# Two layers of attention, mixer and MLP on one core: layer 1 split into a shorter last pair of chunks, value products on four column tiles, late outputs repacked by TensorE

## The chip, the cores and the metric

The kernel runs on one core of a Trainium2 chip. The metric is device time of one execution in microseconds (us); the kernel before takes 1644.31 us (median of 3 runs, 1643.47 to 1644.97). A change of less than 2% counts as "the same". The core's granted TensorE clock was 0.994 to 1.0 of full speed in each profile that the text compares.

## The reference, cut to what matters

```python
def reference(A_x, A_wq, A_wk, A_wv, A_wo, B_x, B_w1, B_w2, B_w3, B_w4):
    # S = 2048 tokens, D = 512, H = 32 query heads of 16, ONE key and value head
    # A: softmax(q k / 4) v, then wo        B: a token-shifting mixer (w1, gelu, shift, w2)
    #                                          and an MLP (w3, gelu, w4) of width 1792
    x = A_x
    x = x + _A_ref(_layernorm(x), A_wq, A_wk, A_wv, A_wo)      # layer 1, attention
    x = x + _B_ref(_layernorm(x), B_w1, B_w2, B_w3, B_w4)      # layer 1, mixer and MLP
    x = x + _A_ref(_layernorm(x), A_wq, A_wk, A_wv, A_wo)      # layer 2, same weights
    x = x + _B_ref(_layernorm(x), B_w1, B_w2, B_w3, B_w4)
    return x
```

Each layer needs 32 x 2048 x 2048 exponentials, which is 1024 units of 128 x 1024, 2048 for both layers. All of layer 1's tokens have to be finished before the last keys of layer 2 exist.

## The kernel before

The program is written by a scheduler that runs when the kernel is built. Operations are declared with what they read and write, an assumed duration and a priority; the scheduler fixes the order in which each engine executes them. The order is then frozen: nothing is decided on the chip. So most of the class constants below are not sizes of the computation but settings of that scheduler.

Queries go in *chunks* of up to four tiles of 128. While the attention of one chunk runs, the *side work* of the chunk before it (output projection, mixer, MLP, keys and queries for layer 2) runs between the attention products. An attention unit has a score product on TensorE (PE), an exponential of 128 x 1024 on ScalarE (ACT, written to `EA`), and a value product on PE. To relieve ACT some units are done by VectorE (DVE) instead. Such a *pair* costs two conversions from PSUM (where TensorE's products land) into the integer tile `J`, two shifted copies `JK`, and three value products:

```python
    # declare_pair (cut)
            o = op("DVE", lambda e, i=i, L=L: e.tensor_scalar(
                out=J[:, i * 512:(i + 1) * 512], in0=self.PB[:, L.bank, :],
                scalar1=128 * LOG2E * 0.25, scalar2=float(127 * 128), op0=ALU.mult, op1=ALU.add), ...)
        for k in (1, 2):
            eng = "POOL" if len(self.adds) < self.ADDS else "DVE"        # ADDS = 0: always DVE
            x = op(eng, lambda e, k=k, r=r: e.tensor_scalar(
                out=self.JK[:, r, :], in0=J, scalar1=float(self.STEPS[k]), scalar2=1.0, ...), ...)
```

A pair is granted while the order is made, when a score product is placed, if enough of the three shared PSUM banks are free and DVE is not behind:

```python
    def attach(self, q):
        if sum(1 for t, b in self.pl.pool if t + 0.06 <= self.pl.now) >= self.FREE:     # FREE = 2
            self.assign(self.pl.now, 1 - q.pe[3][0] // 2)
    # assign (cut): no grant if DVE is too far behind
        if self.pl.backlog() > self.BACKLOG or ...                                      # BACKLOG = 6
```

Value products and most side products use PE in the same tiling (one `pe_kind`), score products in another. While PE is in the first, a side product of that kind gets the priority `STICK` (-1: ahead of everything, unless a due score product would become late), although value products have priority 2 and side products mostly 10:

```python
            if stick and o.prio > 2 and o.pe[0] == self.pe_kind and not any(... > x for x in due):
                key = (self.STICK, o.seq)
```

The value product of a unit, in the kernel before: two heads, each on its own column tile of 32, 512 columns each. `CHUNKS` gives each chunk as (first tile, tiles); `URGE` gives the priority of each chunk's side work, `PACE` spreads that work over time:

```python
    CHUNKS = (((0, 4), (4, 4), (8, 4), (12, 4)),              # layer 1
              ((0, 4), (4, 4), (8, 4), (12, 2), (14, 2)))     # layer 2
    # declare_pv (cut)
                for i in range(2):
                    h = 2 * p + i
                    ins = e.matmul(self.PB[32 * h:32 * h + 32, self.ACC, 0:w], lhsT=v[:, la, kb + j, :],
                                   rhs=ap[:, i, j * w:(j + 1) * w], ..., tile_position=(0, 32 * h))
```

The softmax here doesn't subtract the row's maximum and nothing guards it: scores larger than these inputs give would overflow.

## Time and profile before

| | before | read from |
|---|---|---|
| median time | 1644.3 us | runs |
| exponentials on ACT, and pairs on DVE | 1545 and 503 | groups of instructions (1006 conversions J, two a pair) |
| ACT, DVE, POOL, PE busy | 94%, 86%, 6%, 99% | page, first part |
| start of the first exponential | 19.6 us | trace |
| lost between exponentials | 47.2 us | worked out, see below |
| end of the last exponential to the end (the tail) | 59.0 us | trace |

The lines of these views stand in the prediction. "Lost" is worked out from the trace for each two exponentials that follow one another on ACT: the time from start to start, less 0.917 us (the pitch of an undisturbed row of them), less the GELUs and table loads that lie between (before a GELU, and again before the next exponential, ACT loads a table, 1.28 us each). Added up by stretch it shows where ACT had nothing to do. Because the order is frozen, the number of exponentials can be counted without running anything; how much is lost can't.

The same view by stretch for all engines will be used again. Its columns are the stretch, its length, and for PE, PE's weight loads, DVE, ACT and POOL the busy time (and instructions), then the granted clock, the DMA share and GB/s. Before, in the quiet stretch where only attention runs, and in the one that holds most of the border:

```profile
41.00:205.00 164.00, 163.22 (x1732) 46.41 (x1728) 150.71 (x308) 164.00 (x181) 0.00 (x0) 1.00 0.04 8
...
780.00:960.00 180.00, 175.99 (x2343) 62.17 (x2341) 146.80 (x325) 151.02 (x156) 16.53 (x25) 1.00 0.01 2
```

In the first ACT is never idle. In the second, at the border of the layers, it is idle for 29 us of 180. The longest, on PE and then on ACT:

```profile
789.70 6.43 PE L607 MATMUL PB<-W,G 128*32 128x512 bf16 x116
```
```profile
796.38 30.38 ACT L997 ACTIVATE EA<-PB 128x1024 bf16<-128x1024 f32 x33 [9.64 <-PE PB L1075]
```

PE did MLP products in a row (from 787.31; the first fence shows the part in the view from 790 us), the value products that free EA came after them, and then 33 exponentials ran without a wait. So here ACT did not lack keys or queries: its buffers were full, because side products went ahead of value products. The second longest wait, 7.6 us up to 865.74, has 144 products of the MLP's first layer on PE in the same way.

### The profile page before, as it was taken

To read this page: it belongs to the slowest core of one execution; us is meant where nothing else is said; L and a number is where in the kernel's file an instruction comes from. 1 tells how busy PE (TensorE), PEld (TensorE's weight loads), DVE (VectorE), ACT (ScalarE), POOL (GpSimd) and SP (SyncE) were. 2 spreads that over 40 slices of the span, in tenths; PEclk is the share of its full clock that TensorE was granted. 3 is DMA by queue.
4 is the path that set the end of the run, shared out by engine and by line. 5 is a ranking of instruction groups with operands and counts; after the bars stand their busy time and mean duration, and the time that the engine had idled before them with its cause. 6 is when DMAs were issued, how large, how long until landed. Compare 5 with 4: busy or idle time off the path is not lost.

```text
span 1641.6 us, 47631 instructions
## 1 busy us (share of the span) xinstructions
PE 1617.8 (99%) x21141; PEld 545.5 (33%) x21141; DVE 1414.8 (86%) x2978; ACT 1535.7 (94%) x1623; POOL 105.6 (6%) x162
## 2 busy tenths in 40 slices
PE   8999999999999999999999999999999999999999
PEld 3222223322332223233333332333223223444454
DVE  8999999889999789898986798998899987899853
ACT  4999999999999999999797999999999999999952
POOL 3000000000010001100120000010000000010001
PEclk9999999999999999999999999999999999999999
DMA  6000000000100000100000000000000000000000
GB/s 204 17 4 4 5 18 5 5 3 5 18 5 3 5 3 5 18 5 5 2 2 2 2 8 8 5 18 4 14 11 4 4 5 11 19 5 5 6 17 18
DMA packets 24398, 20.79 MB, mean 13 GB/s; under 512 B 7168, under 2 KB 23680, under 8 KB 24192
## 3 DMA queue, kind: packets, MB, share of 16 engines
q1 hardware_dynamic: 24192, 17.75, 4.1%
q8 instruction: 165, 2.70, 0.7%
q14 instruction: 41, 0.34, 0.1%
HBM read 7.90 MB, written 2.10 MB: 6 GB/s over the span
## 4 chain that ended last, share of the span: by engine, by line
ACT 75%; PE 22%; DVE 2%; DMA 0%; POOL 0%; issue 0%; SPq 0%; POOLq 0%
ACT EA L997 70%; PE PB L607 10%; PE PB L953 6%; PE PB L1075 5%; ACT G L1364 2%; ACT L997 1%; ACT GP L1288 1%; ACT L1288 1%; PE PB L773 1%; ACT L1364 0%; DVE ST L713 0%; DVE G L1357 0%; DVE ZR L756 0%; DMA X<-in_A_x_dram 0%; POOL X L1371 0%; DVE J L1018 0%
## 5 line engine op out<-in xcount | busy, mean ns | idle before, releaser
L997 ACT ACTIVATE EA<-PB 128x1024 bf16<-128x1024 f32 x1545 | 1423.2, 1084 | 58.4 <-PE PB L1075 34.1
L1018 DVE TENSOR_SCALAR J<-PB 128x512 uint16<-128x512 f32 x1006 | 651.0, 683 | 107.5 <-PE PB L953 103.4
L953 PE MATMUL PB<-QT,KT 32*128 32x512 bf16 (+1 forms) x4608 | 623.3, 360 | 9.9 <-ACT EA L997 7.1
L1075 PE MATMUL PB<-EA,VP 128*32 128x512 bf16 (+1 forms) x3482 | 465.6, 362 | 0.9 <-DVE ACCF L1107 0.3
L1028 DVE TENSOR_SCALAR JK<-J 128x1024 uint16<-128x1024 uint16 x1006 | 387.5, 427 | 13.6 <-PE PB L1075 7.6
L953 PEld LDWEIGHTS PB<-QT,KT 32*128 32x128 bf16 x4608 | 159.9, 91 | 565.8 <-ACT EA L997 506.0
L1075 PE MATMUL PB<-JK,VD 128*32 128x512 bf16 (+1 forms) x2252 | 331.8, 361 | 0.2
L1075 PE MATMUL PB<-J,VD 128*32 128x512 bf16 (+1 forms) x1126 | 186.4, 361 | 2.6 <-DVE J L1018 2.6
L607 PE MATMUL PB<-ZT,W 128*32 128x512 bf16 (+2 forms) x2816 | 170.8, 344 | 0.5 <-DVE J L1018 0.4
L1075 PEld LDWEIGHTS PB<-EA,VP 128*32 128x32 bf16 x3482 | 121.3, 94 | 137.7 <-issue 114.6
L607 PE MATMUL PB<-ONES,NIL 128*32 128x512 bf16 x1416 | 143.7, 392 | 4.5 <-DVE ZR L756 1.3
L1075 PEld LDWEIGHTS PB<-JK,VD 128*32 128x32 bf16 x2252 | 90.5, 95 | 107.2 <-issue 54.7
L607 PE MATMUL PB<-W,G 128*32 128x512 bf16 x1792 | 125.2, 382 | 0.3 <-ACT G L1353 0.2
L730 POOL TENSOR_SCALAR SM<-MV 128x4 f32<-128x4 f32 (+3 forms) x30 | 9.6, 319 | 1137.6 <-DVE MV L715 1137.6
L1357 DVE CAST G<-PB 128x512 bf16<-128x512 f32 (+2 forms) x126 | 72.9, 582 | 10.1 <-PE PB L607 8.5
L607 PEld LDWEIGHTS PB<-ZT,W 128*32 128x32 bf16 x2816 | 57.4, 96 | 56.0 <-issue 33.4
L1075 PEld LDWEIGHTS PB<-J,VD 128*32 128x32 bf16 x1126 | 51.0, 95 | 36.1 <-issue 20.1
L1135 DVE TENSOR_TENSOR OS<-ACCF,PB 128x512 bf16<-128x512 bf16 (+1 forms) x72 | 44.7, 621 | 12.6 <-PE PB L1129 8.1
L1364 ACT ACTIVATE G<-G 128x3584 bf16<-128x3584 bf16 (+2 forms) x18 | 46.0, 2601 | 9.8 <-DVE G L1357 9.7
L607 PEld LDWEIGHTS PB<-W,G 128*32 128x32 bf16 x1792 | 37.5, 95 | 46.9 <-issue 26.8
L607 PEld LDWEIGHTS PB<-ONES,NIL 128*32 128x32 bf16 x1416 | 36.0, 96 | 38.5 <-issue 8.0
L1371 POOL TENSOR_TENSOR X<-Y,X 128x512 f32<-128x512 bf16 x32 | 38.4, 1204 | 154.4 <-DVE Y L1326 149.6
(83 smaller groups left out, 824.5 us busy)
## 6 DMA issues: line engine op xcount, KB each, us to landing
W<-in_B_w_dram SPq DMA_DIRECT2D x2, 1792.0 KB, 15.2
OT<-OS SPq DMA_DIRECT2D x224, 16.0 KB, 1.8
QT<-QS SPq DMA_DIRECT2D x40, 64.0 KB, 2.4
X<-in_A_x_dram SPq DMA_DIRECT2D x8, 256.0 KB, 5.2
out_dram<-OUTB SPq DMA_DIRECT2D x16, 128.0 KB, 1.7
W<-in_B_w_dram SPq DMA_DIRECT2D x2, 512.0 KB, 9.0
OT<-OS SPq DMA_DIRECT2D x64, 8.0 KB, 1.8
WQ<-in_A_wq_dram SPq DMA_DIRECT2D x1, 512.0 KB, 4.9
```

Source lines behind the costliest of these rows:

```text
L607: ins = e.matmul(self.PB[32 * g:32 * g + 32, bank, 0:n], lhsT=lhsT[:, 32 * g:32 * g + 32], rhs=rhs, start=start, stop=stop, tile_position= ...
L773: ins = e.transpose(self.PBH[:, L.bank, j * 512 + i * 128:j * 512 + (i + 1) * 128], self.ZR[:, tb % 4, dc * 128:(dc + 1) * 128], self.IDENT)
L953: ins = e.matmul(self.PB[:, bank, j * n:(j + 1) * n], lhsT=self.KT[32 * h:32 * h + 32, la, (kb + j) * 128:(kb + j + 1) * 128], rhs=self.QT ...
L997: o = q.feeds = op("ACT", lambda e: e.activation(self.EA[:, ea, :, :], self.PB[:, b0:b0 + 2, :], ACTF.Exp, scale=0.25), writes=bk + [("EA" ...
L1018: o = op("DVE", lambda e, i=i, L=L: e.tensor_scalar(out=J[:, i * 512:(i + 1) * 512], in0=self.PB[:, L.bank, :], scalar1=128 * LOG2E * 0.25 ...
L1028: x = op(eng, lambda e, k=k, r=r: e.tensor_scalar(out=self.JK[:, r, :], in0=J, scalar1=float(self.STEPS[k]), scalar2=1.0, op0=ALU.add, op1 ...
L1075: ins = e.matmul(self.PB[32 * h:32 * h + 32, self.ACC, 0:w], lhsT=v[:, la, kb + j, :], rhs=ap[:, i, j * w:(j + 1) * w], start=first and j ...
L1135: op("DVE", lambda e: e.tensor_tensor(out=self.OS[:, m, 0:n], in0=acc, in1=self.PB[:, M.bank, 0:n], op=ALU.mult), reads=[("ACCF", m)], wri ...
L1288: op("ACT", lambda e: e.activation(self.GP[:, par, :, 2:2 + n], self.GP[:, par, :, 2:2 + n], ACTF.Gelu_apprx_tanh), reads=gt, writes=gt, d ...
L1357: op("DVE", lambda e, f=f, L=L: e.tensor_copy(self.G2[:, f, 0:n], self.PB[:, L.bank, 0:n]), writes=[L, ("G2", f)], dur=t_ps(n), give=L)
L1364: ins = e.activation(self.G2[:, a:a + 7, 0:n], self.G2[:, a:a + 7, 0:n], ACTF.Gelu_apprx_tanh)
L1371: op("POOL", lambda e, tb=tb: e.tensor_tensor(out=self.X32[:, tb, :], in0=self.Y[:, tb % 6, :], in1=self.X32[:, tb, :], op=ALU.add), reads ...
```

## The change

Its intent: two shorter chunks at the end of layer 1, as layer 2 has them already, so that less side work is left when the attention of layer 1 is through; value products of 256 columns on all four column tiles, meant to take half as much of PE's time; and for the last blocks of a layer a small matmul instead of a DMA to bring outputs into the layout of the output projection. The diff also moves the JK copies to GpSimd (POOL), makes one POOL power of what were two chained roots, and changes many settings. Its core:

```diff
-    CREDIT = 0.15
+    CREDIT = 0.2
-    PATIENCE = 2.0
-    SLACK = 0
-    NEAR_FILL = 0.2
+    PATIENCE = 3.0
+    SLACK = -0.05
+    DMA_LATE = 2.5
+    NEAR_FILL = 0
-    CHUNKS = (((0, 4), (4, 4), (8, 4), (12, 4)),
+    CHUNKS = (((0, 4), (4, 4), (8, 4), (12, 2), (14, 2)),
               ((0, 4), (4, 4), (8, 4), (12, 2), (14, 2)))
-    EARLY = (7, 11)
-    URGE = ((10, 10, 10, 1.5), (10, 10, 10, 10, 10))
+    EARLY = (6, 11)
+    URGE = ((10, 10, 10, 3, 1), (10, 10, 10, 1.5, 10))
-    ADDS = 0
+    ADDS = 6
+    LATE_OT = 4
-    PACE = ((2.8, 2.8, 2.2, 0.3), (2.8, 2.2, 0.5, 0.5, None))
+    PACE = ((2.8, 2.8, 1.5, 0.5, 0.3), (2.8, 2.2, 0.5, 0.5, None))
-    BACKLOG = 6
+    BACKLOG = 1
 ... (CAP, SPARE and QUICK, and how `deferred` gathers value products)
 ... (rstd: two chained POOL roots become DVE operations and one POOL power)
-                for i in range(2):
-                    h = 2 * p + i
-                    ins = e.matmul(self.PB[32 * h:32 * h + 32, self.ACC, 0:w], lhsT=v[:, la, kb + j, :],
-                                   rhs=ap[:, i, j * w:(j + 1) * w], ..., tile_position=(0, 32 * h))
+                for x in range(4):
+                    i, u = divmod(x, 2)
+                    ins = e.matmul(self.PB[32 * x:32 * x + 32, self.ACC, p * hw:p * hw + hw], lhsT=v[:, la, kb + j, :],
+                                   rhs=ap[:, i, j * w + u * hw:j * w + u * hw + hw], ..., tile_position=(0, 32 * x))
 ... (block_end)
+        if c == len(self.CHUNKS[la]) - 1 and b >= self.LATE_OT:
+            (four small matmuls with SELO, then a DVE copy into OT)
+        else:
+            (the DMA, now of eight parts)
```

## The prediction

> **What bounds the kernel now.** I read the page first, then the waits of ScalarE (ACT) by stretch, then the timeline of single engines, then the chain of the last 50 us. On the page:
>
> ```profile
> PE 1617.8 (99%) x21141; PEld 545.5 (33%) x21141; DVE 1414.8 (86%) x2978; ACT 1535.7 (94%) x1623; POOL 105.6 (6%) x162
> ...
> L997 ACT ACTIVATE EA<-PB 128x1024 bf16<-128x1024 f32 x1545 | 1423.2, 1084 | 58.4 <-PE PB L1075 34.1
> L1018 DVE TENSOR_SCALAR J<-PB 128x512 uint16<-128x512 f32 x1006 | 651.0, 683 | 107.5 <-PE PB L953 103.4
> ...
> L1028 DVE TENSOR_SCALAR JK<-J 128x1024 uint16<-128x1024 uint16 x1006 | 387.5, 427 | 13.6 <-PE PB L1075 7.6
> ```
>
> The exponentials are 2048 units of 1024 columns. ACT does 1545 of them; VectorE (DVE) does the other 503, as pairs: two conversions from PSUM (J) and two shifted copies (JK), so (651.0 + 387.5)/503 = 2.06 us of DVE a pair. PE's 99% is no sign of a bound: 1416 of its matmuls (L607, NIL by ONES) are fillers that keep its clock up.
>
> In the waits of ACT, the stretches 41 to 779 us and 945 to 1550 us hold 1.1 us of waiting in all. All that ACT loses lies in three places: before 41 us (24.5 us, the head), at the border of the two layers, and after 1559 us. The waits of ACT from 779 to 945 us:
>
> ```profile
> ACT EA L997 <- PE PB L1075: 28.8, 8, 9.6
> ```
>
> and the last part of the chain that ended last:
>
> ```profile
> 1593.51 0.42 DVE OS L1135
> ...
> 1593.95 0.51 SPq L1140
> ...
> 1595.77 1.79 DMA OT<-OS
> ...
> 1611.77 3.41 POOL X L1371 x3
> ```
>
> So the time is ACT's: a pitch of 0.918 us (75 exponentials in 68.95 us), 1545 of them 1418 us; GELUs and table loads 1535.7 - 1423.2 = 112.5 us; head, border and tail 24.5 + 29 + 51 = 104; the sum is 1635 of 1641.6. Only three things move it: fewer units on ACT, less starving at the border, and a shorter tail. What decides ACT's share is how many pairs DVE gets through. Where nothing else runs (41 to 205 us) there are 70 pairs beside 184 ACT units, 0.38 to one, and DVE is over 90% busy; beside the projections and MLP of a chunk (287 to 780 us) there are 160 pairs beside 515, 0.31.
>
> **What the Trainium skill says.** SBUF — State Buffer, "Who interferes with whom": a VectorE instruction in a 2-port performance mode and a GpSimd instruction exclude one another, while a VectorE instruction with at most one SBUF input outside those modes contends with neither. The trace agrees. Timelines of POOL and DVE at 277 us and at 472 us:
>
> ```profile
> 277.49 1.28 POOL L1371 TENSOR_TENSOR X<-Y,X 128x512 f32<-128x512 bf16 x1 [41.56 <-DVE Y L1326]
> ...
> 472.28 1.16 POOL L1371 TENSOR_TENSOR X<-Y,X 128x512 f32<-128x512 bf16 x1 [5.42 <-DVE Y L1326]
> ```
> ```profile
> 277.33 1.72 DVE L1028 TENSOR_SCALAR JK<-J 128x1024 uint16<-128x1024 uint16 x2
> ...
> 472.20 1.29 DVE L1018 TENSOR_SCALAR J<-PB 128x512 uint16<-128x512 f32 x2
> ```
>
> At 277 us two JK copies take 1.72 us instead of some 0.76, because one waits for POOL; at 472 us two J conversions run beside the same POOL instruction at their usual 1.28. GPSIMD Engine Reference, 3.1: a body of at most two operations runs at 1.03 cycles an element of 1.2 GHz. No large one-input POOL instruction is in this trace. An estimate for 1024 elements is 0.88 us by that page plus the 0.2 to 0.3 us that a 4-element one costs here (L730): 1.1 us. TensorE: Matmul & The Clock Gate, "Wait — 56ns, not 53.3ns?": start to start is N / 2.4 GHz + 2.5 ns and never below about 25 ns. The change makes value products of 256 columns on four tiles, close to that floor. The trace has such a run already, in PE's timeline:
>
> ```profile
> 1586.82 6.30 PE L607 MATMUL PB<-ZT,W 128*32 128x256 bf16 x224
> ```
>
> (6.30 - 0.17 of modelled tail) / 224 = 27.4 ns each, 110 ns for four: full rate, with a weight load before each one. TensorEngine Tiling (Array Packing), "Key Properties": a change of tiling mode drains TensorE. Here each step from scores to values costs about 0.32 - 0.213 = 0.11 us beyond the stream (score products start at 299.81, value products at 300.13).
>
> **The change part by part.**
>
> *Value products.* Each was two matmuls of 512 columns on two tiles (0.22 us, unless a partner of the other two heads was ready); now it is four of 256 on all tiles (0.11 us). For one ACT unit PE needs scores and switch 0.32, value 0.11, switch 0.11 = 0.54 us; a pair adds 3 x 0.11 = 0.33. With 1545 and 503: 834 + 166 us, and about 360 us of projections, MLP and small products from their instruction counts at 55 ns per 512 columns: 1360 of some 1540 us. The old form adds up to 0.11 us for each product without a partner. Where ACT waits for nothing this saves no time by itself; it gives PE room at the border, and for more pairs.
>
> *JK copies.* The few words do not name this, but ADDS goes from 0 to 6: a copy goes to POOL unless six are outstanding, which is nearly always. A pair then costs DVE 651.0/503 = 1.29 us, not 2.06, and POOL 2 x 1.1 = 2.2 us. DVE could do 800 pairs. POOL could do (1540 - 100)/2.2 = 650. The three PSUM banks limit further: a pair is granted at an ACT unit when two of the three are free, so every second unit at best (0.5), and every third when an eviction of side work holds one bank. I take 0.43 in quiet stretches and 0.36 beside side work, 0.37 over all against 0.326 now. Then ACT has 2048/1.37 = 1495 units, 50 fewer: 50 x 0.918 = -46 us. This is the largest and least certain term.
>
> *Two chunks of 256 at the end of layer 1.* At the border PE must now push through outputs, mixer of four tiles and MLP of five. The two MLP products of a tile are 56 matmuls of 512 columns each (1792 of L607 W,G over 32 tiles), at 55 ns together 6.2 us; outputs, W1 and W2 are 16 each, 2.7 us; so 4 x 2.7 + 5 x 6.2 = 42 us. After the split two tiles and three MLPs are left: 24 us. The spilled early blocks of layer 2 run beside it for about 100 us with PE free for some 30% of it, so 24 us fits and 42 does not. I expect 29 us of starving to fall to 7: -22 us. The price: eight more block ends and narrower evictions (256 columns 0.42 us, 512 columns 0.68) and one more GELU pass with two table loads, 2 x 1.28: +5 us.
>
> *Tail.* The repack by TensorE replaces 3.6 us (end of OS 1593.93 to 1597.56) by a matmul and a copy, about 0.9: -2.7. The power of the variance now goes ahead of the three residual additions on POOL: -3. One POOL power instead of two chained roots: -2. Side work of the chunk before is made urgent, so its first MLP product (6.3 us of PE in front of the last block's normalization) should leave the tail: -6. Together -14 us. Head: DVE adds the epsilon, under 1 us.
>
> Sum: 1644.3 - 46 - 22 + 5 - 14 = 1567; the head and the shorter root chains elsewhere may give some 3 us more, so I say 1564.
>
> **Rivals.** *POOL becomes the bound.* If a copy took 1.7 us (two-input instruction rate, 1.17 us for 512), 503 pairs would need 1700 us of POOL, block ends would wait for the last copies, and ACT would starve once its seven EA buffers are full: 1650 or more. For it: no measurement of this form exists. Against it: overflow to DVE after six. *Pairs do not increase*, because banks or the stricter backlog limit (6 to 1 us) hold them at 0.32: then border and tail alone act, 1644 - 31 = 1613. For it: DVE's 103.4 us of waiting for score products shows that not only DVE's own speed limits pairs. *All goes through:* 0.42 overall, 103 us fewer on ACT, no starving: 1644 - 94 - 29 + 5 - 16 = 1510; then POOL would be at 92% and PE above 90%, which I doubt.
>
> **Range and chances.** Border and tail are nearly sure and worth 2% by themselves (1611.4 is the line). The copies add 0 to 90 us with some chance of harm. Range 1520 to 1614. Faster by over 2%: 0.87; within 2%: 0.10; slower: 0.03.
>
> **What would show it.** ACT exponentials near 1495 and J conversions near 1106; JK on POOL at about 1.1 us and hardly any on DVE; POOL busy above 70%, DVE under 80%; value products 128x256 only, four in 0.11 us; ACT's wait at the border under 10 us; no DMA of OT in the final chain and about 45 us from the last exponential to the end (59 now). The prediction is wrong if ACT waits for value products of JK all along, if POOL copies are near 1.7 us, or if the count of exponentials stays at 1545.

## More of the kernel before

`FREE` (2) and `STICK` (-1) are not in the diff: both kernels have them.

## The result, and the profile after

The changed kernel takes 1642.39 us (median of 4 runs, 1642.28 to 1642.92); the kernel before took 1644.3 on the same chip (1643.47 to 1644.97). The ratio is 0.9989, with an interval of 0.9972 to 1.0007: the same. Ratios here are the mean time of one kernel's runs over that of the other's of the same rounds, so they are not quite the ratio of the medians that are quoted beside them. The prediction said 1564, with 1520 to 1614 as its range.

The lines of the page that answer to those of before:

```profile
PE 1588.0 (97%) x31269; PEld 676.6 (41%) x31269; DVE 1181.5 (72%) x2130; ACT 1530.5 (93%) x1606; POOL 1172.1 (71%) x1143
...
L990 ACT ACTIVATE EA<-PB 128x1024 bf16<-128x1024 f32 x1525 | 1415.3, 1085 | 55.8 <-PE PB L946 39.7
L1021 POOL TENSOR_SCALAR JK<-J 128x1024 uint16<-128x1024 uint16 x1039 | 1087.9, 1047 | 368.8 <-DVE J L1011 237.8
L1011 DVE TENSOR_SCALAR J<-PB 128x512 uint16<-128x512 f32 x1046 | 675.7, 684 | 241.3 <-PE PB L946 237.4
...
L609 PE MATMUL PB<-ONES,NIL 128*32 128x512 bf16 x2316 | 200.3, 387 | 6.4 <-DVE ZR L749 3.0
```

Everything that the change moves has moved: the copies are on POOL at 1.047 us each, DVE has fallen from 86% to 72%, POOL risen from 6% to 71%. Yet only 20 exponentials have left ACT (1545 to 1525). DVE's new room is idle time before the conversions, waiting for score products: 237.4 us where it was 103.4. And part of PE's new room went to the fillers (ONES, NIL: products of constants that the scheduler puts in where PE would idle): 2316 where there were 1416.

The waits of ACT from 779 to 945 us (what waited for what: us in total, times, longest), and below them the longest one from 945 to 1550:

```profile
ACT G L1378 <- DVE G L1371: 5.9, 1, 5.9
ACT EA L990 <- PE PB L1069: 3.9, 3, 2.6
ACT EA L990 <- PE PB L946: 1.7, 2, 1.2
```
```profile
ACT EA L990 <- PE PB L946: 15.9, 1, 15.9
```

At first sight the border has improved: 11.5 us where 28.8 stood. But the waiting has only moved past 945 us, into one wait of 15.9 us for score products: together 27.4 us. And this longest wait is of another kind than those before: it ended with a score product, right after the last keys of layer 2 were written (KT, 951.28 us), so now ACT does run out of keys. From 41 to 779 us, where ACT waited for 1.1 us in all, there is now this, above all:

```profile
ACT EA L990 <- PE PB L1069: 8.7, 7, 2.9
```

The two stretches of before, after (engines in the same order; POOL is the fifth):

```profile
41.00:205.00 164.00, 157.94 (x2656) 60.35 (x2656) 111.66 (x184) 161.49 (x177) 145.27 (x140) 1.00 0.04 8
...
780.00:960.00 180.00, 172.13 (x2990) 74.28 (x2987) 128.69 (x251) 152.80 (x158) 104.66 (x106) 0.99 0.01 2
```

In the quiet stretch DVE's load fell from 151 to 112 us, but POOL is busy for 145 of 164 us. It did 140 copies there and DVE 5, beside 146 conversions, so 73 pairs, where DVE alone had managed 70. One nearly full engine took the place of another.

The ledger of the two profiled executions (1641.6 and 1640.7 us) closes to 0.1 us:

| | us, after less before |
|---|---|
| 20 exponentials fewer, 0.917 each | -18.3 |
| GELUs and table loads | +2.7 |
| lost between exponentials, 47.2 to 60.0 | +12.8 |
| first exponential, 19.6 to 20.5 | +0.9 |
| after the last exponential, 59.0 to 59.9 | +0.9 |
| sum (measured difference of the spans: -0.9) | -1.0 |

Within the lost time: before 41 us it fell from 6.7 to 3.5, from 41 to 574 it rose from 0.8 to 5.8, from 574 to 780 us from 0.9 to 12.7, at the border (780 to 960) it fell from 30.0 to 28.8, from 960 to 1559 it rose from 3.3 to 8.8, and after that it fell from 5.3 to 0.5.

### The profile page after: what moved, and what is told of

Same layout as the page of the kernel before. It is cut to its first block, busy times and chain, and to the rows that moved or that the text cites. A ratio compares the mean times of both kernels' runs of the same rounds, so it can differ in the third digit from the quotient of the medians. Undisturbed runs are those within 1.5% of the kernel's fastest.

```text
span 1640.7 us, 68466 instructions
## 1 busy us (share of the span) xinstructions
PE 1588.0 (97%) x31269; PEld 676.6 (41%) x31269; DVE 1181.5 (72%) x2130; ACT 1530.5 (93%) x1606; POOL 1172.1 (71%) x1143
## 4 chain that ended last, share of the span: by engine, by line
ACT 65%; PE 30%; DVE 3%; DMA 1%; POOL 0%; SPq 0%; issue 0%; POOLq 0%
ACT EA L990 61%; PE PB L609 12%; PE PB L946 9%; PE PB L1069 8%; ACT G L1378 2%; ACT L990 1%; DVE J L1011 1%; PE PB L766 1%; ACT GP L1302 1%; ACT L1302 0%; ACT L1378 0%; DVE G L1371 0%; DVE ZR L749 0%; SPq L1152 0%; PE PB L808 0%
## 5 line engine op out<-in xcount | busy, mean ns | idle before, releaser
L990 ACT ACTIVATE EA<-PB 128x1024 bf16<-128x1024 f32 x1525 | 1415.3, 1085 | 55.8 <-PE PB L946 39.7
L1021 POOL TENSOR_SCALAR JK<-J 128x1024 uint16<-128x1024 uint16 x1039 | 1087.9, 1047 | 368.8 <-DVE J L1011 237.8
L1011 DVE TENSOR_SCALAR J<-PB 128x512 uint16<-128x512 f32 x1046 | 675.7, 684 | 241.3 <-PE PB L946 237.4
L1069 PE MATMUL PB<-EA,VP 128*32 128x256 bf16 (+1 forms) x7660 | 388.3, 255 | 1.9 <-DVE KT L1087 0.5
L1069 PE MATMUL PB<-JK,VD 128*32 128x256 bf16 (+1 forms) x5160 | 280.7, 257 | 4.4 <-POOL JK L1021 3.5
L1069 PEld LDWEIGHTS PB<-EA,VP 128*32 128x32 bf16 x7660 | 166.6, 95 | 175.7 <-issue 147.8
L609 PE MATMUL PB<-ONES,NIL 128*32 128x512 bf16 x2316 | 200.3, 387 | 6.4 <-DVE ZR L749 3.0
L1069 PEld LDWEIGHTS PB<-JK,VD 128*32 128x32 bf16 x5160 | 116.2, 95 | 127.8 <-issue 73.7
L1069 PE MATMUL PB<-J,VD 128*32 128x256 bf16 (+1 forms) x2580 | 149.5, 255 | 2.3 <-DVE J L1011 1.1
L609 PEld LDWEIGHTS PB<-ZT,W 128*32 128x32 bf16 x2880 | 66.9, 96 | 27.4 <-issue 12.4
L1069 PEld LDWEIGHTS PB<-J,VD 128*32 128x32 bf16 x2580 | 60.5, 96 | 41.3 <-issue 25.4
L742 POOL TENSOR_TENSOR SM<-SM,MH 128x4 f32<-128x4 f32 (+4 forms) x32 | 32.6, 1018 | 57.0 <-DVE SM L734 32.3
L1129 DVE TENSOR_TENSOR OS<-ACCF,PB 128x512 bf16<-128x512 bf16 (+1 forms) x80 | 46.0, 575 | 20.8 <-PE PB L1123 20.5
L609 PEld LDWEIGHTS PB<-W,G 128*32 128x32 bf16 x1792 | 43.2, 96 | 23.4 <-issue 6.0
L1101 DVE CAST ACCF<-PB 128x512 bf16<-128x512 f32 (+1 forms) x73 | 41.4, 567 | 10.3 <-PE PB L1069 10.1
```

What stands on the lines that cost most here:

```text
L609: ins = e.matmul(self.PB[32 * g:32 * g + 32, bank, 0:n], lhsT=lhsT[:, 32 * g:32 * g + 32], rhs=rhs, start=start, stop=stop, tile_position= ...
L742: op("POOL", lambda e: e.tensor_tensor(out=self.SM[:, 0:k, a:b], in0=self.SM[:, 2:2 + k, a:b], in1=self.MH[:, 0:k, a:b], op=ALU.pow), read ...
L990: o = q.feeds = op("ACT", lambda e: e.activation(self.EA[:, ea, :, :], self.PB[:, b0:b0 + 2, :], ACTF.Exp, scale=0.25), writes=bk + [("EA" ...
L1011: o = op("DVE", lambda e, i=i, L=L: e.tensor_scalar(out=J[:, i * 512:(i + 1) * 512], in0=self.PB[:, L.bank, :], scalar1=128 * LOG2E * 0.25 ...
L1021: x = op(eng, lambda e, k=k, r=r: e.tensor_scalar(out=self.JK[:, r, :], in0=J, scalar1=float(self.STEPS[k]), scalar2=1.0, op0=ALU.add, op1 ...
L1069: ins = e.matmul(self.PB[32 * x:32 * x + 32, self.ACC, p * hw:p * hw + hw], lhsT=v[:, la, kb + j, :], rhs=ap[:, i, j * w + u * hw:j * w + ...
```

## The experiments

18 kernels ran, each for three rounds beside the kernel before (which took 1643.8 to 1644.3 us). "Lost" is the time lost between exponentials, 60.0 us in the changed kernel.

**1. Copies back on DVE.** Edit to the changed kernel:

```diff
-    ADDS = 6
+    ADDS = 0
```

> The changed kernel with the JK copies back on VectorE and nothing else altered. Its program has 1546 exponentials on ScalarE (changed kernel 1525). Theory (number of exponentials sets the time): 21 x 0.917 = 19 us longer than the changed kernel, about 1661 us. Rival (the places where ScalarE waits set it, and moving the copies only trades one for the other): within 8 us of 1642. VectorE should be near 87% busy again and the normalizing copies that now wait for GpSimd (0.95 and 0.81 us each) back near 0.54 and 0.40.

Measured: 1651.5 us (1648.8 to 1653.9), ratio 1.0046; 1546 exponentials, lost 51.7 us. The copies on POOL are worth 9 us in this kernel, although they take 21 exponentials (19 us) off ACT. The mechanism is there and small, and half of it is paid back in waiting.

**2. Grant more pairs.**

```diff
-    FREE = 2
+    FREE = 1
```

> The changed kernel, but a pair is granted when one of the three shared PSUM banks is free instead of two. Its program has 1468 exponentials, 57 fewer than the changed kernel. Theory that the number of exponentials sets the time: 57 x 0.917 = 52 us faster, about 1590 us. Rival (pairs take banks from the projections and the MLP, which then come late, and ScalarE waits for them at the border of the layers and inside the layers): not faster than the changed kernel, 1640 to 1680 us, with ScalarE waiting over 50 us more than the changed kernel between 41 us and its last exponential.

Measured: 1662.2 us (1661.0 to 1666.5), ratio 1.0116, with 57 exponentials *fewer* than the changed kernel. The group of exponentials:

```profile
L990 ACT ACTIVATE EA<-PB 128x1024 bf16<-128x1024 f32 x1468 | 1364.3, 1061 | 124.2 <-PE PB L1069 72.9
```

ACT's busy time with them fell by 51 us, and its idle time before them more than doubled, 72.9 us of it released by value products (L1069). An exponential needs a free EA buffer, and a buffer comes free when its value product is done. Lost: 141.3 us. So the theory that only the number of exponentials matters is refuted: the pairs can be had for the asking, but they are paid back, and more, in waiting.

**3. The split undone in the changed kernel.** Urgencies, paces and `EARLY` of layer 1 go back with it:

```diff
-    CHUNKS = (((0, 4), (4, 4), (8, 4), (12, 2), (14, 2)),
+    CHUNKS = (((0, 4), (4, 4), (8, 4), (12, 4)),
-    EARLY = (6, 11)
+    EARLY = (7, 11)
```

> The changed kernel with layer 1 ending in one chunk of 512 again (and the early keys, urgencies and paces that belong to it). 1512 exponentials. If the split shortens the border as predicted (22 us less waiting), this one waits some 20 us more there and is about 1650 us. Rival: the border stays between 25 and 35 us either way, the losses in the 256-wide chunks of layer 1 (some 12 us between 574 and 780 us) go, 13 exponentials fewer are worth 12 us, and it is equal or faster: 1625 to 1645 us.

Measured: 1650.4 us, ratio 1.0038; 1512 exponentials, lost 95.6 us, of it 35.2 at the border, 34.2 from 960 to 1559 us and 12.2 after that. With these settings the split is worth 8 us. The first theory's 1650 us was met, but not by its mechanism: the border lost only 6.4 us more than with the split, where 20 were expected, and 25.4 us more were lost from 960 to 1559. Experiment 11 against 8, and 17 against 15, show that the worth holds for these settings only.

**4. Keys of layer 2 made early.** The keys of the last tiles are made from the attention's output, before mixer and MLP (wrong, though the difference stayed within the tolerance of the comparison). The call that makes keys is moved ahead of the mixer in `chunk_end` for the last chunk of layer 1.

> The changed kernel, but in the last chunk of layer 1 the keys and values of layer 2 are made before the mixer and the MLP, from rows that are not finished: wrong results on purpose. 1521 exponentials. Theory (ScalarE waits 16 us at 952 us because it has used up all work whose keys exist, and the last keys stand behind MLP, normalization and projection): this wait goes, and with it 12 to 20 us of the time if nothing takes its place. Rival (the border is short of TensorE time or banks, not of keys): the waiting between 780 and 990 us stays above 20 us in other places, and the time within 5 us of 1642.

Measured: 1645.5 us (1643.0 to 1646.3), ratio 1.0007; 1521 exponentials. Lost from 780 to 960 us fell from 28.8 to 9.8, but from 960 to 1395 it rose to 22.4 (14.1 + 8.3) and after 1559 to 9.9. GELUs and table loads between exponentials also grew by 5.9 us, and the tail shrank by 9.2. So taking the wait away saved nothing here. My reading is that the side work has to get through PE at some point, and without the wait it is in the way later; the run shows the sum, not that reason.

**5. Four-tile value products alone, in the kernel before.** The new `declare_pv` with the layout of outputs that goes with it; no split, no copies on POOL, no repacking, settings of before.

> The kernel before with the value products on four tiles and nothing else of the change (the copies stay on VectorE, layer 1 is not split, all settings as before). 1536 exponentials against 1545. Theory (TensorE is not what ScalarE waits for inside the layers, so its freed time turns into fillers and idling): value products stream 80 to 100 us less, the [...]fillers rise from 354 groups to about 570, and the time moves by no more than the 9 exponentials are worth, 1633 to 1645 us. Rival (TensorE time is the bound): 20 us or more faster.

Measured: 1649.7 us, ratio 1.0034; 1536 exponentials, lost 54.6 us, and 65.6 us after the last exponential. The share of PE's time from 41 to 1559 us that goes to value products fell from 0.294 to 0.233 (reconstructed from the starts in the trace), and fillers and idle time took it. The time lies 5 us above the range of the theory, although exponentials fell by 9; far from the rival. PE's room alone is worth nothing where ACT and DVE set the pace.

**6. Two-tile value products in the changed kernel** (and so no repacking, which is made for the new layout).

> The changed kernel with the value products back on two tiles (no repack by TensorE, which needs the new layout), all else as changed. 1523 exponentials against 1525. If the four tiles are worth nothing by themselves: within 8 us of 1642. If copies on GpSimd and the split live off the TensorE time that the four tiles free: 20 to 40 us slower, 1662 to 1682 us, with ScalarE waiting for value products in the layers.

Measured: 1673.7 us (1672.9 to 1674.2), ratio 1.0178; 1523 exponentials, lost 94.3 us, of it 48.8 at the border. The same part that was worth nothing in experiment 5 is worth 31 us here, together with the repacking that needs it: beside the new pairs and the new order PE is needed.

**7. Residual additions out of the tail's chain.** In the tail, POOL's additions wait until DVE's normalizing copies are made.

```diff
-                reads=[("Y", tb % 6)], writes=[("X", tb)], dur=1.3, port=True)
+                reads=[("Y", tb % 6)] + ([("ZR", t % 4) for t in tiles] if tail else []),
+                writes=[("X", tb)], dur=1.3, port=True)
```

> The changed kernel, but the three residual additions on GpSimd in the last chunk wait for the normalizing copies, so that the power of the variance goes ahead of them, as I had predicted that the change would do. The exponentials stay 1525. Theory: the 3.4 us of additions leave the last chain, 2 to 3.5 us faster than the changed kernel, about 1639.5 us. Rival: TensorE's order or the shared port takes it back, within 1 us of it.

Measured: 1642.7 us, ratio 0.9987: no gain. The chain that ended last (start, duration, what) shows why. In the changed kernel, and then in this one:

```profile
1611.76 3.41 POOL X L1385 x3
...
1615.23 0.91 POOLq L464
```
```profile
1610.65 1.29 DVE Y L1340 x2
...
1613.21 1.17 DVE ST L720 x2
...
1614.88 0.86 POOL SM L742
```

The additions had stood in the chain because they were in POOL's queue ahead of the power. Without them the power starts at 1614.88 where it was 1615.23, since DVE's statistics come no earlier. A row of the chain is worth only the distance to the next thing that ends.

**8. The changed kernel, retuned.** The operations of the changed kernel with other settings, found by a search that varied them in the kernel's own scheduler. The search knows nothing of the chip but the scheduler's assumed durations, so this run was a test of its choice.

```diff
-    CREDIT, FORCE, BUNCH, PATIENCE, SLACK = 0.2, 0.6, 2, 3.0, -0.05
+    CREDIT, FORCE, BUNCH, PATIENCE, SLACK = 0.25, 0.5, 3, 4.0, 0
-    DMA_LATE, NEAR_FILL, STICK, FREE, BACKLOG, ADDS = 2.5, 0, -1, 2, 1, 6
+    DMA_LATE, NEAR_FILL, STICK, FREE, BACKLOG, ADDS = 0, 0.2, None, 1, 0.5, 5
-    CHUNKS of layer 1: 4, 4, 4, 2, 2 tiles; EARLY = (6, 11)
+    CHUNKS of layer 1: 4, 4, 4, 4 tiles; EARLY = (7, 11)
     and HOLD, LATE_OT, QUICK, URGE, PACE
```

> The code of the changed kernel with other settings only: layer 1 not split, pairs granted at one free bank but only while VectorE has less than 0.5 us of side work waiting, side work of the late chunks paced faster, value products gathered in threes, copies overflow to VectorE after five. 1489 exponentials, which is about the number that my prediction had. Theory (the four tiles and the copies on GpSimd are worth what I predicted, some 40 to 50 us, but the settings of the changed kernel spend it as waiting and fillers): 1590 to 1615 us, with less than 35 us of waiting between the first and the last exponential. Rival (each further pair comes back as waiting whatever the settings, as when pairs were granted at one free bank): 1635 us or more.

Measured: 1603.2 us (1602.3 to 1603.5), ratio 0.9749. This version is correct and beats both kernels, by 41 us. From its page:

```profile
PE 1558.2 (97%) x28693; PEld 660.9 (41%) x28693; DVE 1257.8 (79%) x2238; ACT 1494.5 (93%) x1567; POOL 1159.6 (72%) x1125
...
L989 ACT ACTIVATE EA<-PB 128x1024 bf16<-128x1024 f32 x1489 | 1382.5, 1067 | 54.6 <-PE PB L1068 27.2
...
L608 PE MATMUL PB<-ONES,NIL 128*32 128x512 bf16 x1588 | 138.6, 390 | 7.0 <-DVE ZR L748 2.0
```

It has 36 exponentials fewer than the changed kernel, and its ACT waits no longer before them (54.6 us, 55.8 in the changed kernel). Lost: 57.6 us, 29.0 of it at the border; after the last exponential 59.4. (The theory's time range held; its "less than 35 us of waiting" did not.) So nearly all the gain is exponentials: 36 x 0.917 = 33 of the 39 us between the two kernels. These exponentials were taken off ACT without new waiting. So the prediction's largest term existed, and the changed kernel's own settings had left it unused. Experiments 10 to 18 take this apart.

**9. Copies half as long on POOL.** Each copy writes 512 of its 1024 columns (wrong: relative error 0.147), and the order is made for 0.6 us a copy.

> The changed kernel, but each copy on POOL writes only the first 512 of its 1024 columns (the result is wrong on purpose; the rest is zero from the start), and the schedule is made for 0.6 us a copy where it was 1.05. The schedule then holds 1500 exponentials on ACT, 25 fewer. Theory (the time of a copy on POOL, 2.1 us a pair, is what keeps the number of pairs down): 25 x 0.917 = 23 us less, 1615 to 1625 us, and more than 70 pairs in the quiet stretch from 41 to 205 us. Rival (pairs are paid back in waiting, because TensorE's share and the PSUM banks set the pace): within 6 us of the changed kernel, 1636 to 1648, with ACT losing over 75 us between exponentials where the changed kernel loses 60.

Measured: 1643.2 us (1637.0 to 1644.9), ratio 0.9987; lost 90.1 us. A copy took 0.62 us. In the quiet stretch:

```profile
41.00:205.00 164.00, 159.27 (x2729) 61.80 (x2725) 118.11 (x193) 162.77 (x179) 96.28 (x156) 1.00 0.05 10
```

There are 158 conversions, 79 pairs where the changed kernel has 73, and POOL is far from full: in this stretch POOL had held the pairs down (so had the grant rule: experiments 2 and 15, with full copies, have 76). But the whole program gains nothing from 25 exponentials fewer; it loses 30 us more in waiting, with 12.0 from 205 to 369 us and 23.4 from 1395 to 1559 (1.3 and 2.3 in the changed kernel). The rival holds: POOL's speed is not what bounds the changed kernel.

**10. Copies back on DVE in the retuned kernel** (`ADDS` 5 to 0).

> The retuned kernel (1603.2 us, 1489 exponentials) with all JK copies back on DVE; the schedule holds 1530 exponentials. Theory (with fitting settings the copies on POOL are worth what the prediction's largest term said, nearly all of it): 41 x 0.917 = 38 us more, 1635 to 1643 us, and DVE above 84% busy. Rival (as inside the changed kernel, where half of the 21 exponentials saved was lost to waiting): 1618 to 1628.

Measured: 1633.8 us (1631.6 to 1634.9), ratio 0.9935; 1530 exponentials, lost 50.4 us. The copies on POOL are worth 30.6 us here, of the 38 that 41 exponentials make. In the changed kernel they were worth 9. The time is just under the range that I had given the theory (1635 to 1643), and 6 us above the rival's.

**11. The split put into the retuned kernel.**

```diff
-    CHUNKS of layer 1: 4, 4, 4, 4 tiles
+    CHUNKS of layer 1: 4, 4, 4, 2, 2 tiles, with an urgency and a pace for the fifth chunk
```

> The retuned kernel with layer 1 split again into chunks of 4, 4, 4, 2 and 2 tiles (the retuned one has four chunks of 4 there). The schedule holds 1484 exponentials, 5 fewer. Theory of the prediction (the split shortens the starving at the border): 15 to 25 us less, 1578 to 1590. My theory now (the split does not shorten what is left at the border, because the short chunk's side work queues behind that of the chunk before, and it adds waits from 574 to 780 us): 10 to 40 us more, 1613 to 1643, with the border's loss no lower than 25 us.

Measured: 1631.6 us (1630.5 to 1635.4), ratio 0.9927; 1484 exponentials, lost 89.2 us. The border loses 56.6 us where the retuned kernel loses 29.0. The prediction's theory falls. (No search was made for settings that suit the split in this order, so 28 us is its price with these settings.) The timeline of ACT shows the order of events. The retuned kernel's GELUs (GP is the mixer's, G the MLP's), with what was waited for in brackets:

```profile
822.10 1.91 ACT L1301 ACTIVATE GP<-GP 128x2048 bf16<-128x2048 bf16 x1
...
864.94 4.78 ACT L1377 ACTIVATE G<-G 128x2688 bf16<-128x2688 bf16 x2
...
894.12 3.29 ACT L1377 ACTIVATE G<-G 128x1792 bf16<-128x1792 bf16 x2 [4.25 <-DVE G L1370]
```

and the same kernel with the split:

```profile
797.56 3.17 ACT L1377 ACTIVATE G<-G 128x3584 bf16<-128x3584 bf16 x1
...
844.49 1.06 ACT L1301 ACTIVATE GP<-GP 128x1024 bf16<-128x1024 bf16 x1
...
874.48 3.29 ACT L1377 ACTIVATE G<-G 128x1792 bf16<-128x1792 bf16 x2
...
911.97 1.06 ACT L1301 ACTIVATE GP<-GP 128x1024 bf16<-128x1024 bf16 x1
...
935.91 4.78 ACT L1377 ACTIVATE G<-G 128x2688 bf16<-128x2688 bf16 x2 [12.83 <-DVE G L1370]
```

Unsplit there is one passage mixer, MLP at the border. Split there are two, and the second mixer comes behind the first MLP: the last mixer GELU at 912 instead of 822 us. And the MLP of the chunk before (the pass with 3584 columns) has only just ended, at 800 us.

**12. The old structure, as long searched.** In the changed kernel's code: two-tile value products, copies on DVE, four chunks of 4, no repacking, with the settings that a search like that of experiment 8 found.

> The parts of the change undone in the changed kernel's code (value products on two tiles, no copies on POOL, layer 1 in four chunks of 4, no repacking by TensorE), with settings chosen by a search as long as that for the retuned kernel. The schedule holds 1521 exponentials. Theory (the retuned kernel's gain needs the parts of the change: four tiles and copies on POOL): 1630 to 1645 us, so no or little gain over before. Rival (the settings alone make the gain, the parts are worth nothing): 1600 to 1615.

Measured: 1629.6 us (1629.0 to 1630.5), ratio 0.991; 1521 exponentials. It lies just under the range of my theory and outside the rival's. So of the retuned kernel's 41 us some 15 are had without these parts, by settings and by the small changes that this code shares with the changed kernel (the POOL power, the MLP's waits), and 26 come with the parts, with no split among them. (That the two searches were equally long is said, not shown.)

**13 and 14. One setting put back in the retuned kernel each.**

```diff
# 13
-    STICK = None
+    STICK = -1
# 14
-    FREE = 1
+    FREE = 2
```

> The retuned kernel (1603.2 us, 1489 exponentials) with one setting put back: TensorE stays with a kind of side product once begun, ahead of value products and of all but scores (STICK -1). The schedule holds 1480 exponentials, 9 fewer. Theory (this rule makes value products wait, the buffers between ScalarE and TensorE fill, and pairs are paid back in waiting): 30 us or more above the retuned kernel, 1635 to 1680, with over 60 us lost between exponentials beyond the retuned kernel's 58. Rival (the rule hardly matters; what counts is the number of exponentials): 1590 to 1605.

> The retuned kernel with another setting put back: a pair is granted only when two of the three PSUM banks are free, not one (FREE 2). The schedule holds 1536 exponentials, 47 more. Theory (granting limits the pairs, and the pairs pay fully in the retuned order): 47 x 0.917 = 43 us more, 1640 to 1652. Rival (the additional pairs were half paid back in waiting): 1618 to 1630.

Measured: 13 took 1677.3 us (1675.1 to 1678.3), ratio 1.0198 (unclear against the 2% line), with 1480 exponentials; 14 took 1648.5 us (1648.0 to 1649.7), ratio 1.0026, with 1536. The groups of exponentials, 13 and then 14:

```profile
L989 ACT ACTIVATE EA<-PB 128x1024 bf16<-128x1024 f32 x1480 | 1373.9, 1077 | 134.9 <-PE PB L1068 102.4
```
```profile
L989 ACT ACTIVATE EA<-PB 128x1024 bf16<-128x1024 f32 x1536 | 1424.9, 1074 | 51.1 <-PE PB L945 26.4
```

These two are the clearest pair. Number 13 has fewer exponentials than any other kernel here but number 2, and yet it is the slowest of all, 74 us above the retuned kernel: ACT stands idle before them for 134.9 us, 102.4 of it until a value product ended. That is what the rule does, it lets side products pass the value products that free EA. Number 14 has no such waiting (lost 53.7 us); it just has 47 exponentials more, 43 us, and is 45 us slower. So in this order `FREE` sets how many pairs there are, and `STICK` whether ACT can profit from them. Experiment 2 had changed one without the other. (The other settings were chosen for `STICK` off, so 74 us is what the rule costs in this order; `STICK` off alone in the changed kernel was not run.)

**15. Both put into the changed kernel,** with the backlog limit of experiment 8, and nothing else:

```diff
-    FREE = 2; STICK = -1; BACKLOG = 1
+    FREE = 1; STICK = None; BACKLOG = 0.5
```

> The changed kernel with three settings changed and nothing else: a pair granted at one free bank (FREE 1), no staying with side products (STICK off), and the backlog limit for grants 0.5 instead of 1 us. The schedule holds 1492 exponentials, 33 fewer. Theory (the changed kernel held its own gain back by granting too late and by letting side products go ahead of value products; these two settings together suffice): 33 x 0.917 = 30 us less, 1608 to 1620. Rival (the split and the rest of the settings eat it, as granting alone did): 1635 to 1660.

Measured: 1636.3 us (1633.5 to 1636.9), ratio 0.9946; 1492 exponentials, lost 84.5 us. That is in the rival's range, at its lower edge; the theory falls. From 41 to 780 us the loss is now 9.4 us (31.5 in experiment 2), but the border alone loses 57.5 (54.9 in experiment 2, 28.8 in the changed kernel) and the tail is 69.4 us. What the pairs gain is mostly given back at the border and after.

**16. Keys early in the retuned kernel** (the edit of experiment 4; wrong in the same way).

> The retuned kernel with the keys of layer 2 for the last tiles made from layer 1's attention output directly, before mixer and MLP (the result is wrong on purpose). The schedule holds 1495 exponentials, 6 more. Theory of the prediction (starving at the border is lost time): the border's 29 us fall below 10 and the time by 20 us, to 1578 to 1590. Rival (the side work has to be done anyway, and the waiting moves): border below 15 us but the time within 8 us of the retuned kernel, 1595 to 1611, with the loss showing up after 960 us or in the tail.

Measured: 1602.95 us, ratio 0.9748, against 1603.2 for the retuned kernel. The border lost 21.1 us, so less fell away than either side had said; and the 8 us that did were made up by 6 more exponentials (5.5 us) and 5 us of waiting elsewhere, less a tail 3 us shorter. The time did not follow the border, but with so small a step and a new number of exponentials this is weaker than experiment 4.

**17. Three causes together.** The changed kernel with the settings of experiment 15 and layer 1 unsplit as in experiment 3.

> The changed kernel with only these altered: layer 1 in four chunks of 4 with the urgencies and paces of before, a pair granted at one free bank, no staying with side products, backlog limit 0.5 us. Copies on POOL, four-tile value products, repacking and all else as in the changed kernel. The schedule holds 1483 exponentials. Theory (these three held the gain back): 1600 to 1620 us, with the border's loss at 27 to 33 us where the split form of the same settings loses 57. Rival (the other settings of the retuned kernel are needed as well): 1628 to 1645.

Measured: 1625.1 us (1620.9 to 1633.3), ratio 0.9884; 1483 exponentials, lost 84.8 us, 54.0 of it at the border. My theory fell here: the three are not enough, and an unsplit layer can lose as much at the border as a split one. The time lies between the two ranges. The three make 17 of the retuned kernel's 39 us against the changed kernel. The timeline of ACT's GELUs shows what is different from experiment 8. First number 17, then the retuned kernel, the passes of the MLP of tiles 7 to 10, the last before the border:

```profile
781.52 6.27 ACT L1378 ACTIVATE G<-G 128x3584 bf16<-128x3584 bf16 x2
```
```profile
728.44 6.27 ACT L1377 ACTIVATE G<-G 128x3584 bf16<-128x3584 bf16 x2
```

The side work that comes before the border is 53 us later, at the same number of exponentials within 6. Over the kernels with `FREE` 1 and `STICK` off (16, with its early keys, left out) the border's loss goes with this time: 728 us and 34 us lost from 697 to 960 (experiment 8), 731 and 33 (10), 758 and 50 (18), 779 and 59 (15), 782 and 56 (17), 794 and 58 (11). The kernel before, whose attention reaches the border later, has this MLP at 769 us and loses 30. Which of the remaining settings makes the side work early I did not isolate. The pace of that chunk's side work is a candidate (third number of `PACE`: 0.5 in the retuned kernel, 2.2 in number 17), but it can't be all: number 11 has 0.5 too, and its MLP is the latest.

**18. Two-tile value products in the retuned kernel.**

> The retuned kernel (1603.2 us) with value products on two tiles (and, as the layout of the outputs then differs, no repacking by TensorE). The schedule holds 1496 exponentials, 7 more, worth 6 us. Theory (TensorE's freed time is what lets 559 pairs run beside the side work; without it they are paid back in waiting): 30 to 60 us more, 1633 to 1663, the loss between exponentials 30 us or more above 58. Rival (four tiles matter little once the order is right): 1608 to 1618.

Measured: 1664.5 us (1661.1 to 1666.0), ratio 1.0119; 1496 exponentials, lost 100.1 us. Just above the theory's range. Of it 42 us are more waiting and 18 a longer tail (77.6 us). Four tiles, with the repacking that needs them, are worth 61 us in this order. Since the settings were chosen for four tiles, this is more than an old structure with settings of its own would lose (experiment 12).

## Why the prediction was wrong, point by point

**What bounds the kernel.** The first step was right: ACT sets the time, and the ledger of both kernels closes on ACT. What it left out is that ACT's waiting is not a property of the three places where it was seen. Experiments 2 and 13 have 124 and 135 us of idle time before exponentials, where the kernel before has 58. Some of its counts were off without consequence: from 41 to 205 us ACT has 181 exponentials and not 184, from 287 to 780 us 499 and not 515 (0.39 and 0.32 pairs to one). Nor does DVE's "800 pairs" follow from its numbers (1540 us less 376 of other work, at 1.29 us, is 900), nor a rival's 1.7 us a copy from 1.17 us for 512 columns (at that rate it is 2.3).

**Value products.** Right in size: the trace of the changed kernel has groups of four that start 0.12 us before the next product (100.48 and 100.60 us), and the share of PE's time from 41 to 1559 us fell from 0.294 to 0.235, 90 us. Right too that this "saves no time by itself": experiment 5.

**JK copies.** The costs were right: 1.047 us for a copy (1.1 was said), 675.7/523 = 1.29 us of DVE a pair, POOL at 71%, DVE at 72%. The step that failed is "I take 0.43 in quiet stretches and 0.36 beside side work, 0.37 over all". The runs gave 523/1525 = 0.343. In the quiet stretch it was nearly right: 73 pairs beside 177, 0.41. Beside side work it failed: from 287 to 780 us there are 160 pairs beside 485 exponentials, 0.33, and the kernel before had the same 160. So the term was -18 us and not -46. In the quiet stretch POOL was nearly full (145 of 164 us busy; 79 pairs when copies were halved), with the grant rule close behind (76 pairs at one free bank). Beside side work it was the grant rule: at one free bank the retuned kernel has 180 pairs beside 492 from 287 to 780 us, 0.37, and with the rule put back (experiment 14) 160 again. The prediction knew the rule and guessed how often it would be met; experiment 14 measures it, 47 exponentials between a threshold of two free banks and one. And a higher count would not have been enough: in the order that `STICK` makes, the rival "ACT would starve once its seven EA buffers are full" comes true, though not because POOL is slow as that rival had it, but because side products pass the value products. (`BACKLOG`, stricter in the change, was not tested by itself.) The prediction's -46 us can be had from the same operations (1489 exponentials are 36 fewer than the changed kernel's and 56 fewer than before), and the changed kernel did not have it.

**Two chunks of 256.** Two steps failed. The first is the wait: "29 us of starving". The kernel before did not starve at the border; its 28.8 us are waits for value products, 17 of them behind the two rows of side products described above. A shorter row needs another order, not only less side work for the last chunk. The second is "After the split two tiles and three MLPs are left". Side work of the chunk before was still in the queue when the short chunk's attention was over. In the changed kernel the attention of tiles 12 and 13 ended some 95 us after the chunk before, and the side work of a chunk of four takes about 200 us. From the last output projection of the border to the last keys it took 155 us; before, 158. Now ACT did starve: 15.9 us for the last keys. ACT's timeline in the changed kernel:

```profile
810.10 1.06 ACT L1302 ACTIVATE GP<-GP 128x1024 bf16<-128x1024 bf16 x1
...
852.18 3.28 ACT L1378 ACTIVATE G<-G 128x1792 bf16<-128x1792 bf16 x2
...
891.25 1.06 ACT L1302 ACTIVATE GP<-GP 128x1024 bf16<-128x1024 bf16 x1
...
930.30 4.78 ACT L1378 ACTIVATE G<-G 128x2688 bf16<-128x2688 bf16 x2 [5.87 <-DVE G L1371]
952.33 8.36 ACT L990 ACTIVATE EA<-PB 128x1024 bf16<-128x1024 f32 x9 [15.95 <-PE PB L946]
```

All four tiles of mixer and five of MLP lie after 796 us, in two passages one behind the other. The last mixer GELU is at 891 us; in the kernel before the only one is at 828. So the term was -1 us and not -22. The value of the term is doubtful too: experiments 4 and 16 take away waiting at the border by other means (19 and 8 us) and the time does not fall.

**The price of the split** was put at +5. GELUs and table loads cost 2.7, but the waits from 574 to 780 us cost 11.8 more, where the short chunk's attention and side work lie. That is not the split alone: unsplit (experiment 3) 4.0 us are lost there, split with `STICK` off 4.4 (experiment 15) or 10.1 (experiment 11). By experiment 3 the split is nevertheless worth 8 us with the changed kernel's settings; in experiment 17 against 15 it costs 11, in the retuned kernel 28. In this kernel it has no worth apart from the settings around it.

**Tail.** Only one of the four parts came true: no DMA of OT is in the chain. The additions on POOL were worth 0.35 us and not 3 (experiment 7). "Its first MLP product should leave the tail" did not happen: just before the last block's copy from PSUM, the chain of the changed kernel still has

```profile
1584.15 3.90 PE PB L609 x88
...
1588.87 0.42 DVE G L1371
...
1594.12 0.44 DVE ACCF L1101
```

(with eleven more such casts G between the last two), which is that MLP. One power in place of two roots shortened the chain by little: from the additions' start to the power's end it took 4.58 us before and 4.38 now, 0.2 us less where 2 were expected. The term was +0.9 us and not -14.

**Rivals and chances.** The second rival, "Pairs do not increase", came nearest on the pairs, but it too counted border and tail as nearly sure. That was the mistake in the chances: 31 us were treated as firm because their waits could be pointed at in the profile. None of them was a wait of which it had been shown that the time follows.

**What stays open.** The retuned kernel's remaining 22 us over number 17 come with the earlier side work, by the times given there; I have not shown which setting does it, and the relation between that time and the border's loss rests on these few kernels. The worth of the repacking by TensorE was not measured by itself, and neither was what it costs that DVE's normalizing operations became slower (last section). `STICK` off alone and `BACKLOG` alone in the changed kernel, and a split with settings searched for it, were not run.

## What to carry to other kernels

When work is taken off the engine that sets the time, look at two things before counting it: what rule decides how much is taken, and what order the released engine's partners work in, because the gain goes into waiting if what frees its buffers is queued behind less urgent work. A wait that can be seen is not yet time that can be saved; read what ended it, and try a run that takes it away by any means, even with a wrong result, and see whether the end moves. A structural change and the settings around it belong together: compare both structures after an equal search for settings, or the comparison measures the search.

## What the Trainium skill lacked or had wrong

- GPSIMD Engine Reference, 3.1: its rate for small bodies led to a good estimate (1.1 us), but it has no figure for a large one-input 16-bit instruction. Measured: 1.047 us for 128x1024 and 0.620 for 128x512 on average, so 0.83 ns a column ((1047 - 620)/512) and about 0.19 us of fixed cost; the page's 1.03 cycles at 1.2 GHz would be 0.86 ns.
- SBUF — State Buffer, "Who interferes with whom": nothing wrong; the case agrees, with sizes that depend on the kernel and so cannot stand there. With POOL at 71% in place of 6%, DVE's normalizing operations went from 403 to 805 ns (ZR from Y, MV and SM) and from 342 to 713 ns (ZR from Y and SM), and back to 402 and 341 with the copies on DVE again (experiment 1), while the conversions from PSUM stayed at 683 and 684 ns. The prediction had named the rule and left this out of its sum.
- TensorEngine Tiling (Array Packing), "Key Properties": it says that a change of tiling mode drains TensorE, without a duration. Here a step between score products and products of the other tiling costs about 0.10 us beyond the stream, at 0.213 us for 512 columns as in the prediction (medians 0.102 one way and 0.099 back, in both kernels). From 41 to 1559 us there are 3065 such steps before and 3030 after, so an estimate is 0.20 of PE's time, nearly as much as the value products.
- No page that I read says what a seen wait is worth: experiments 4 and 16 removed 19 and 8 us of waiting at the border, and the times changed by +3 and -0.2 us.
